# Query and key projections: the last 64 rows' high products of two tiles as one pair of half-height matmuls

## The chip, the cores and the metric

The kernel runs on one core of a Trainium2 chip. The metric is the device time of one launch in microseconds, as the median of several runs. A profiled execution of the same kernel gives the trace from which all durations below are taken.

## The reference, cut to what matters

Two independent computations stand side by side in the output, `[2048, 2 x 576]`. The left half is an attention with a compressed memory over four segments of 512 positions; the right half is a two-dimensional Fourier transform written as matrix products.

```python
# A: x [1, 2048, 576], H = 32 heads of Dh = 18, N = 4 segments of L = 512
q, k, v = x @ wq, x @ wk, x @ wv            # split by head and segment
for s in range(N):
    p = softmax(qs @ ks.T * scale + mask)   # mask: -1e9 where key > query
    a_dot = p @ vs
    a_mem = phi(qs) @ M / (phi(qs) @ z + 1e-6)   # phi(t) = t + 1 or exp(t)
    outs.append(g * a_mem + (1 - g) * a_dot)
    M = M + phi(ks).T @ vs;  z = z + phi(ks).sum()
A = concat(outs) @ wo
# B: real part of the transform along both axes
a, b = x2 @ dft_hid_re.T, x2 @ dft_hid_im.T
B = dft_seq_re @ a - dft_seq_im @ b
```

Everything is float32. The change touches the first line alone, the products for q and k.

## The kernel before

**Two parts to a number.** A float32 operand is cut in two: a high part rounded to the format that TensorE reads in one pass (`F32R`), and a low part, the rest. A product of two operands is then three matmuls: high x high, high x low and low x high. ScalarE (`act`) makes the high part, VectorE (`dve`) or GpSimd (`pool`) subtracts for the low one.

**Projections.** The contraction is 576 rows long: four blocks of 128 rows and a tail of 64. q and k are made transposed, in nine tiles of 128 features for each segment (`m` 0 to 3 are q, 4 to 7 are k, 8 holds the last 64 features of both), each tile 128 x 512 in one PSUM bank. A tile is a chain of 14 matmuls (`qk_terms`, L221): 3 for each of the four blocks, and 2 for the tail. The 64 tail rows lie twice in the 128 partitions, once in the upper and once in the lower half. `x_tail` holds high over low; the weights come as low over high (`W[2]`) and high over low (`W[3]`), so that the two matmuls of full height give all four products of the tail.

**Order of the work.** All instructions of an engine run in the order in which the program issues them, and `later(n, ...)` and `tick()` put steps behind. For each of the four segments:
- `open_qk(s)` (L237) runs tiles 0 to 3 side by side in four of the five banks of the tag `acc`, in groups of terms. In segment 0, where the inputs are still arriving, the groups are small; later there are two, terms 0 to 5 and 6 to 13. Between them stand the last sums of the memory (`accumulate`, L358).
- `memory()` (L367) copies the sums of the memory on ScalarE.
- `project_qk(s, m)` (L258) evacuates a tile or, for tiles 4 to 8, first runs its chain (`chain`, L82) in the next of the five banks. The order is 0 to 8 in segment 0 and 0, 1, 2, 3, 8, 4, 5, 6, 7 after that. To evacuate: for k, a copy kept for the memory (`kf`, L266, in segments 0 to 2); the first bfloat16 part `p` (ScalarE, L270); the rest `r` (VectorE, L271); for q, in later segments, `phi` with relu and exp (ScalarE, L214, L215), VectorE's L217 and L218 and GpSimd's L219. The second and third part of `p` (L280 to L283) follow one tick later. A bank comes free with its last reader.
- `project_v(s, j)` makes v in four blocks of positions, with two groups of matmuls each. In segments 0 to 2, between the two groups, TensorE transposes the copies of k (`k_natural`, kt at L300: tiles 8, 4, 5, and then 6 and 7). In segments 1 to 3 the lookups in the memory (`look`, L391 to L399) stand between them too.
- `split_x(s, k)` (L110) cuts the x of the next segment in two; `split_wk` (L119) does it for weights.

**The second part**, from about 220 us on, mixes the attention by heads with the dense products of the Fourier transform, and ends with the product with wo. The change does not touch it.

**Memory.** The pool `sk` lies on the right side of SBUF and is closed in the middle of segment 3, where `sr` takes its place.

Of the kernel before, what the change touches and what calls it, by code (L numbers as in the profile page):

```python
# [12 lines left out]
F32 = mybir.dt.float32  # L13
F32R = mybir.dt.float32r
F16 = mybir.dt.float16
BF16 = mybir.dt.bfloat16
AF = mybir.ActivationFunctionType
OP = mybir.AluOpType
AX = mybir.AxisListType.X
PSUM = bass.MemoryType.PSUM  # L20
DRAM = bass.MemoryType.DRAM

S, D, H, DH, NSEG, L = 2048, 576, 32, 18, 4, 512
P = 128
# [16 lines left out]
def infini_attention_and_fnet(ctx: ExitStack, tc: tile.TileContext, xT, wqk, w8, wv, wo, beta, xtT, cT, hT, out):  # L41
    nc = tc.nc
    act, dve, pool, pe = nc.scalar, nc.vector, nc.gpsimd, nc.tensor
# [14 lines left out]
    def split(hi, lo, raw, lo_engine=None):  # L58
        act.activation(hi, raw, AF.Copy)
        (lo_engine or dve).tensor_tensor(lo, raw, hi.bitcast(F32), OP.subtract)  # L60
# [19 lines left out]
    def chain(o, terms):  # L80
        for n, (a, b) in enumerate(terms):
            pe.matmul(o, a, b, start=n == 0, stop=n == len(terms) - 1)  # L82
# [3 lines left out]
    def later(n, fn, *a):  # L86
        due.setdefault(clock[0] + n, []).append((fn, a))
# [8 lines left out]
    sk = p1k.enter_context(tc.tile_pool(name="sb1k", bufs=1, side="right", reuse_waits="tile"))  # L96
    sb = p1.enter_context(tc.tile_pool(name="sb1", bufs=1, reuse_waits="tile"))
    ps = p1.enter_context(tc.tile_pool(name="ps1", bufs=2, space=PSUM))
# [11 lines left out]
    def split_x(s, k):  # L110
        raw = XR.pop((s, k))
        if k < 4:
            split(X[s][0][k], X[s][1][k], raw)
        else:
            t = X[s][2]
            act.activation(t, raw, AF.Copy)
            dve.tensor_tensor(t[64:], raw[64:], t[64:].bitcast(F32), OP.subtract)

    def split_wk(w, k, raw, wait=0):  # L119
# [14 lines left out]
    def load_w(src, cols, k):  # L134
        raw = sb.tile([P, cols], F32, name="raw", tag="raw", bufs=5)
        dma(raw, src[k])
        return raw

    def weight(mk):
        return [[mk() for _ in range(4)] for _ in range(2)] + [mk() for _ in range(2)]  # L140

    def wide_tile(cols):
        return lambda: wide.tile([P, cols], F32R, name="wide", tag="wide")

    WQ = weight(wide_tile(L))
    x_early = [[[sb.tile([P, L], F32R, name=f"x{n}{k}{i}") for k in range(2)] for n in "hl"] for i in range(2)]
    x_late = [[sb.tile([P, L], F32R, name=f"x{n}{k}") for k in (2, 3)] for n in "hl"]
    x_tail = sb.tile([P, L], F32R, name="xt")
    X = [(x_early[s % 2][0] + x_late[0], x_early[s % 2][1] + x_late[1], x_tail) for s in range(NSEG)]

    load_x(0, 0)
    raw = sb.tile([P, L], F32, name="raw", tag="raw", bufs=5)
# [6 lines left out]
    for k in range(1, 5):  # L159
        load_x(0, k)  # L160
        raw = load_w(wqk[:, :, :L], L, k)
# [3 lines left out]
    WK, WV = weight(wide_tile(L)), weight(wide_tile(D))  # L165
    for k in range(5):
        if k < 2:
            raw = sb.tile([P, L], F32, name="r", tag="r", bufs=3)
            dma(raw, wqk[k, :, L:])
        else:  # L170
            raw = load_w(wqk[:, :, L:], L, k)
# [40 lines left out]
    def phi(e, sources, hi, lo):  # L212
        for to, src in sources:
            act.activation(to, src, AF.Relu, scale=-1.0)  # L214
        act.activation(e, e, AF.Exp, scale=-1.0)  # L215
        for to, src in sources:
            dve.scalar_tensor_tensor(to, src, 0.0, to, op0=OP.max, op1=OP.add)  # L217
        dve.tensor_copy(hi, e)  # L218
        pool.tensor_tensor(lo, e, hi.bitcast(F32), OP.subtract)  # L219

    def qk_terms(s, m):  # L221
        xh, xl, xt = X[s]
        W, c = (WQ, m) if m < 4 else (WK, m - 4) if m < 8 else (W8, 0)
        cs = slice(c * P, (c + 1) * P)
        terms = []
        for k in range(4):
            terms += [(W[0][k][:, cs], xh[k]), (W[0][k][:, cs], xl[k]), (W[1][k][:, cs], xh[k])]
        return terms + [(W[2][:, cs], xt), (W[3][:, cs], xt)]

    FIRST, KF = {}, {}  # L230

    def warm_up():
        o = ps.tile([P, L], F32, name="warm", tag="acc", bufs=5)
# [3 lines left out]
    def open_qk(s):  # L237
        for m in range(4):
            FIRST[m] = ps.tile([P, L], F32, name="qk", tag="acc", bufs=5)
        terms = [qk_terms(s, m) for m in range(4)]  # L240
        edges = (0, 6, 14) if s else (0, 1, 2, 3, 6, 9, 14)
        for a, b in zip(edges, edges[1:]):
            for m in range(4):
                for n in range(a, b):
                    pe.matmul(FIRST[m], *terms[m][n], start=n == 0, stop=n == 13)  # L245
                if s and m == 0 and a:
                    accumulate(3, (1,))
            if s and a == 0:
                accumulate(3, (0,))
# [8 lines left out]
    def project_qk(s, m):  # L258
        if m in FIRST:
            o = FIRST.pop(m)  # L260
        else:
            o = ps.tile([P, L], F32, name="qk", tag="acc", bufs=5)
            chain(o, qk_terms(s, m))
        if m >= 4 and s < 3:
            KF[m] = sk.tile([P, L], F32, name="kf", bufs=5)
            act.activation(KF[m], o, AF.Copy)  # L266
        p = sb.tile([P, 3, L], BF16, name="p", tag="p", bufs=5)
        r = sb.tile([P, L], F32, name="r", tag="r", bufs=3)
        p0, p1, p2 = (p[:, 2 - i] if 4 <= m < 8 else p[:, i] for i in range(3))
        act.activation(p0, o, AF.Copy)  # L270
        dve.tensor_tensor(r, o, p0, OP.subtract)  # L271
        if s and (m < 4 or m == 8):
            n = P if m < 4 else 64
            c = m if m < 4 else 4
            e = sb.tile([P, L], F32, name="qe", bufs=2)[:n]
            phi(e, ((e, o[:n]),), pq_hi[:n, c], pq_lo[:, c] if m < 4 else pq_hi[64:, c])

        def rest():
            if m in (5, 6, 7):
                pool.tensor_copy(p1, r)  # L280
            else:
                act.activation(p1, r, AF.Copy)
            pool.tensor_tensor(p2, r, p1, OP.subtract)  # L283
            if m < 8:
                later(1, dma, (qd if m < 4 else kd)[s][(m % 4) * P:(m % 4 + 1) * P, :3], p)
            else:
                later(1, dma, qd[s][4 * P:, :3], p[:64])
                for i in range(3):
                    later(1, dma, kd[s][4 * P:, 2 - i], p[64:, i])

        later(1, rest)
# [12 lines left out]
    def project_v(s, j, meanwhile):  # L304
        xh, xl, xt = X[s]
        js = slice(j * P, (j + 1) * P)
# [36 lines left out]
    def accumulate(j, which=(0, 1)):  # L343
        (kh, kl), v = kn[j % 2], vn[j % 2]
        for n in which:
            for c in range(5):
                b, at, both = SUMS[c]
                o = sums(c)
                fs = slice(64 + c * P, 64 + (c + 1) * P) if c < 4 else slice(0, 64)
                hs = slice(HEAD0[c] + 8 - o.shape[2], HEAD0[c] + 8)  # L350
                if n:
                    todo = ((kl, v[:, 0, hs], o[:, 0]),)
                elif both:
                    todo = ((kh, v[:, :, hs], o),)
                else:
                    todo = ((kh, v[:, i, hs], o[:, 0]) for i in range(2))
                for keys, values, to in todo:
                    pe.matmul(to, keys[:, fs], values, start=b not in started, stop=True, skip_group_check=True)  # L358
                    started.add(b)
# [135 lines left out]
    for s in range(NSEG):  # L495
        more = s < 3
        if s == 0:
            warm_up()
        open_qk(s)
        if s:  # L500
            memory()
        else:
            tick()
        for n, m in enumerate((0, 1, 2, 3, 8, 4, 5, 6, 7) if s else range(9)):
            project_qk(s, m)
            tick()
            if not more and n in (5, 7):
                h_split(0, (n - 5) // 2)
            if s and n < 8:
                copy_parts(s - 1, 2 * n)  # L510
                copy_parts(s - 1, 2 * n + 1)
            if s in (1, 2) and n >= 4:
                load_x(s + 1, n - 4)
            if not more and n == 0:
                for k in range(5):
                    h_load(0, k)
            if not more and n == 4:
                p1k.close()
                sr = ctx.enter_context(tc.tile_pool(name="sb2r", bufs=1, side="right", reuse_waits="tile"))
                attention_tiles()  # L520
            if not more and n == 4:
                c_load(0)
                c_load(1)
                stacks(sr, 0)
                stack_load(0)
            if not more and n == 6:
                c_load(2)
# [26 lines left out]
    ps = ctx.enter_context(tc.tile_pool(name="ps2", bufs=2, space=PSUM, reuse_waits="tile"))  # L554
# [445 lines left out]
    for t in range(NT):  # L1000
# [3 lines left out]
        for h in range(2):  # L1004
            cs = slice(h * 288, h * 288 + 288)
            o = ps.tile([P, 288], F32, name="d", bufs=3)
            terms = []
# [5 lines left out]
            if h or t == NT - 1:  # L1013
                cs = cs if t == NT - 1 else slice(0, D)
# [45 lines left out]
```

## Time and profile before

| | |
|---|---|
| median of 3 runs | 999.67 us (999.23 to 1004.48) |
| profiled execution | 1000.37 us, its span 998.6 us |
| granted TensorE clock | 0.999 |
| TensorE busy | 989.0 us of the span |
| VectorE, ScalarE, GpSimd busy | 753.9, 710.9, 635.5 us |

A row of the profile names the engine, the line, and output<-inputs with their shapes. PE is a matmul, PEld the load of its weights, DVE is VectorE, ACT is ScalarE and POOL is GpSimd. In a timeline the columns are start and duration in us; a bracket gives the idle time of the engine ahead of the instruction, and who ended it. Several instructions of one kind may be merged in a row (x2). The segments' openings start at 5.1, 58.1, 112.9 and 169.6 us.

### The profile page before, as it was taken

The numbers are of one execution on the slowest core, as the hardware profiler recorded it, in microseconds if no ns is written. First come the engines' busy times: TensorE is split into PE (matmuls) and PEld (weight loads), VectorE is DVE, ScalarE is ACT, GpSimd is POOL, SyncE is SP. The second block draws the span as 40 slices with busy tenths as digits, with TensorE's granted clock in tenths as the row PEclk, the third lists the DMA queues.
The fourth block names the chain that finished last, engine by engine and source line by source line (L and its number), as shares of the span: only waits on it lengthen the run. The fifth ranks groups of instructions, "written<-read, shape, count | busy, mean of one in ns | idle before, by whom it ended". The sixth has DMA issues, their size and how long they took to land.

```text
span 998.6 us, 25575 instructions
## 1 busy us (share of the span) xinstructions
PE 989.0 (99%) x9291; PEld 923.7 (93%) x9291; DVE 753.9 (75%) x2048; ACT 710.9 (71%) x1677; POOL 635.5 (64%) x700
## 2 busy tenths in 40 slices
PE   9999999999999999999999999999999999999998
PEld 7988989898999999999999999999999999999998
DVE  6657668594678777878898888898888899998321
ACT  6667576663887877878788788877767777777243
POOL 2657576686767667666766777776767767767000
PEclk9999999999999999999999999999999999999999
DMA  7447556787578898899999887789999999899555
GB/s 254 161 131 231 205 177 238 236 306 214 138 169 204 208 230 210 209 229 217 254 228 247 220 208 198 181 197 223 223 239 214 242 237 243 228 202 189 137 152 138
DMA packets 305182, 208.92 MB, mean 209 GB/s; under 512 B 206240, under 2 KB 259872, under 8 KB 305056
## 3 DMA queue, kind: packets, MB, share of 16 engines
q1 hardware_dynamic: 304816, 207.15, 80.2%
q8 instruction: 73, 1.20, 0.5%
q14 instruction: 53, 0.43, 0.1%
q10 hardware_dynamic: 240, 0.14, 0.1%
HBM read 121.32 MB, written 57.93 MB: 180 GB/s over the span
## 4 chain that ended last, share of the span: by engine, by line
PE 89%; DVE 3%; DMA 3%; ACT 2%; POOL 2%; issue 1%; SPq 0%; POOLq 0%; DVEq 0%; ACTq 0%
PE d L572 39%; PE s L733 7%; PE d L82 6%; PE v L82 6%; PE pv L851 4%; PE qk L245 4%; PE qk L82 3%; PE d L617 3%; PE d L618 3%; PE d L619 3%; PE pv L852 2%; PE m L358 1%; PE t L807 1%; PE look L391 1%; PE t L810 1%
## 5 line engine op out<-in xcount | busy, mean ns | idle before, releaser
L739 DVE CUSTOM_DVE_ANT_0 s<-s,causal 128x128 f32<-128x128 f32 (+3 forms) x512 | 249.8, 498 | 101.1 <-PE s L733 92.0
L451 POOL TENSOR_TENSOR clo<-craw,chi 128x512 fp32r<-128x512 f32 x158 | 215.9, 1366 | 96.6 <-ACT chi L446 68.0
L572 PE MATMUL d<-wide,chi 128*128 128x288 f32 x1408 | 266.2, 306 | 0.4 <-DVE y L642 0.4
L572 PEld LDWEIGHTS d<-wide,chi 128*128 128x128 f32 x1408 | 211.8, 189 | 2.4 <-DVE y L642 0.6
L572 PE MATMUL d<-wide,clo 128*128 128x288 f32 x704 | 177.6, 319 | 0.0
L773 POOL TENSOR_TENSOR hl<-pf,hl 128x768 f16<-128x768 f32 x64 | 112.7, 1761 | 69.8 <-ACT hl L769 53.9
L733 PE MATMUL s<-ks,qs 108*128 108x128 bf16 (+3 forms) x512 | 133.7, 304 | 1.9 <-DVE negm L739 1.7
L819 ACT ACTIVATE phi<-t 128x384 f16<-128x384 f32 x128 | 61.7, 482 | 103.2 <-PE t L816 103.0
L762 ACT ACTIVATE pf<-s,nb 128x128 f32<-128x128 f32 (+3 forms) x256 | 128.1, 526 | 6.2
L834 DVE TENSOR_TENSOR plo<-pf,phi 128x384 f16<-128x384 f32 (+1 forms) x128 | 126.8, 991 | 0.0
L572 PE MATMUL d<-ab,chi 128*128 128x288 f32 x640 | 126.0, 306 | 0.0
L572 PEld LDWEIGHTS d<-wide,clo 128*128 128x128 f32 x704 | 118.6, 189 | 1.6
L446 ACT ACTIVATE chi<-craw 128x512 fp32r<-128x512 f32 x160 | 100.2, 627 | 5.8 <-DMA craw<-xtT 2.5
L820 ACT ACTIVATE pf<-t 128x384 f32<-128x384 f32 (+1 forms) x192 | 99.5, 518 | 6.2 <-PE t L807 6.0
L572 PEld LDWEIGHTS d<-ab,chi 128*128 128x128 f32 x640 | 98.5, 189 | 0.6
L769 ACT ACTIVATE hl<-pf 128x768 f16<-128x768 f32 (+1 forms) x128 | 87.4, 730 | 2.0
L572 PE MATMUL d<-ab,clo 128*128 128x288 f32 x320 | 84.8, 314 | 0.0
L617 PE MATMUL d<-wide,chi 128*128 128x288 f32 x256 | 84.0, 328 | 0.0
L619 PE MATMUL d<-wide,clo 128*128 128x288 f32 x256 | 75.6, 295 | 0.0
L618 PE MATMUL d<-wide,chi 128*128 128x288 f32 x256 | 75.6, 295 | 0.0
L773 DVE TENSOR_TENSOR hl<-pf,hl 128x512 f16<-128x512 f32 x64 | 67.6, 1056 | 0.1
L834 POOL TENSOR_TENSOR plo<-pf,phi 128x384 f16<-128x384 f32 x64 | 59.4, 928 | 13.0 <-ACT pf L820 10.4
(203 smaller groups left out, 2497.9 us busy)
## 6 DMA issues: line engine op xcount, KB each, us to landing
craw<-cT SPq DMA_DIRECT2D x128, 256.0 KB
ks<-kd SPq DMA_DIRECT2D x32, 432.0 KB
qs<-qd SPq DMA_DIRECT2D x32, 432.0 KB
craw<-xtT SPq DMA_DIRECT2D x32, 320.0 KB
vd<-vs SPq DMA_DIRECT2D x16, 440.0 KB
vst<-vd SPq DMA_DIRECT2D x32, 220.0 KB
qd<-p SPq DMA_DIRECT2D x16, 384.0 KB
kd<-p SPq DMA_DIRECT2D x16, 384.0 KB
```

Of the source, the lines that this page charges most:

```text
L82: pe.matmul(o, a, b, start=n == 0, stop=n == len(terms) - 1)
L446: act.activation(hi, raw[:, :4], AF.Copy)
L451: engine.tensor_tensor(lo, raw[:, :4], hi.bitcast(F32), OP.subtract)
L572: pe.matmul(o[h], a, b[:, h * 288:h * 288 + 288], start=start, stop=stop)
L617: pe.matmul(o, xh[:, k], wl[k][:, cs], start=k == 0, stop=False)
L618: pe.matmul(o, xh[:, k], wh[k][:, cs], start=False, stop=False)
L619: pe.matmul(o, xl[:, k], wh[k][:, cs], start=False, stop=False)
L733: pe.matmul(o[:, c:c + w], q[:, i * P:w], k[:, :w], start=True, stop=True)
L739: dve.tensor_tensor_reduce(o[:, c:c + w], o[:, c:c + w], CAUSAL[0][:, L - w:], scale=scale, scalar=-LOWEST, op0=OP.add, op1=OP.min, accum_ ...
L762: act.activation(f[:, FIRST_COL[i]:FIRST_COL[i] + w], o[:, c:c + w], AF.Exp, bias=nb[:, i:i + 1], scale=-1.0)
L773: engine.tensor_tensor(hl[:, 1, a:b], f[:, a:b], hl[:, 0, a:b], OP.subtract)
L834: (pool if kind == 2 else dve).tensor_tensor(lo[:, a:b], f[:, a:b], hi[:, a:b], OP.subtract)
```

## The change

For tiles 0 to 7 the second tail matmul is dropped as a matmul of full height. Its high x high product is formed with 64 rows instead: for the even tile of a pair in the upper half of the array (`W[3]` and `x_tail`, rows 0 to 63), for the odd tile in the lower half (`W[2]` and `x_under`, rows 64 to 127). The two stand next to each other in the program and write to different banks. The product low x low of the tail is left out for these tiles. `x_under` is a new tile in `sk` that holds the high part of the tail in its lower half; ScalarE copies it for each segment.

In `open_qk` the pair comes after the odd tile's other terms, so tile 0 ends together with tile 1, and 2 together with 3. For tiles 4 to 7 of segments 0 to 2 the pair comes first, ahead of the even tile's 13 other terms; the odd tile's bank is taken at the same time, and its 13 terms follow when its turn comes. In segment 3 the tiles 4 to 7 run as before, with 14 terms, and tile 8 does so in every segment.

```diff
@@ split_x
             act.activation(t, raw, AF.Copy)
+            act.activation(x_under[64:], raw[64:], AF.Copy)
             dve.tensor_tensor(t[64:], raw[64:], t[64:].bitcast(F32), OP.subtract)
@@
+    x_under = sk.tile([P, L], F32R, name="xu")
@@
+    def qk_tails(s, ms, o, first):
+        for n, m in enumerate(ms):
+            W, c = (WQ, m) if m < 4 else (WK, m - 4)
+            cs = slice(c * P, (c + 1) * P)
+            rows, w, x = (slice(64, P), W[2], x_under) if n else (slice(0, 64), W[3], X[s][2])
+            pe.matmul(o[n], w[rows, cs], x[rows], start=first, stop=not first)
+
+    FIRST, KF, PAIRED = {}, {}, set()
+
+    def finish(o, terms):
+        for n in range(13):
+            pe.matmul(o, *terms[n], start=False, stop=n == 12)
@@ open_qk
-                for n in range(a, b):
-                    pe.matmul(FIRST[m], *terms[m][n], start=n == 0, stop=n == 13)
+                for n in range(a, min(b, 13)):
+                    pe.matmul(FIRST[m], *terms[m][n], start=n == 0, stop=False)
+                if b == 14 and m % 2:
+                    qk_tails(s, (m - 1, m), (FIRST[m - 1], FIRST[m]), False)
@@ project_qk
             o = FIRST.pop(m)
+            if (s, m) in PAIRED:
+                finish(o, qk_terms(s, m))
         else:
             o = ps.tile([P, L], F32, name="qk", tag="acc", bufs=5)
-            chain(o, qk_terms(s, m))
+            terms = qk_terms(s, m)
+            if m in (4, 6) and s < 3:
+                FIRST[m + 1] = ps.tile([P, L], F32, name="qk", tag="acc", bufs=5)
+                qk_tails(s, (m, m + 1), (o, FIRST[m + 1]), True)
+                finish(o, terms)
+                PAIRED.add((s, m + 1))
+            else:
+                chain(o, terms)
```

More of the change, by code (lines that the diff above doesn't have):

```diff
@@ L228, in qk_terms @@
         return terms + [(W[2][:, cs], xt), (W[3][:, cs], xt)]
-    FIRST, KF = {}, {}
+    def qk_tails(s, ms, o, first):
[8 more added lines that the diff above has]
+            pe.matmul(o, *terms[n], start=False, stop=n == 12)
     def warm_up():
```

## The prediction

> **What bounds the kernel now.** I read the page first: its engines and the chain of work that ended last.
>
> ```profile
> PE 989.0 (99%) x9291; PEld 923.7 (93%) x9291; DVE 753.9 (75%) x2048; ACT 710.9 (71%) x1677; POOL 635.5 (64%) x700
> PE 89%; DVE 3%; DMA 3%; ACT 2%; POOL 2%; issue 1%; SPq 0%; POOLq 0%; DVEq 0%; ACTq 0%
> PE d L572 39%; PE s L733 7%; PE d L82 6%; PE v L82 6%; PE pv L851 4%; PE qk L245 4%; PE qk L82 3%; PE d L617 3%; PE d L618 3%; PE d L619 3%; PE pv L852 2%; PE m L358 1%; PE t L807 1%; PE look L391 1%; PE t L810 1%
> ```
>
> TensorE is busy throughout and carries 89% of the chain; the lines that are changed (qk at L245 and L82) carry 7%. Busy matmuls overlap in these records, so the next question was whether TensorE really never waits while the projections run. The waits of PE in the first 300 us answer that, and the table of windows does for what follows:
>
> ```profile
> PE warm L235 <- POOL ident L64: 1.4, 1, 1.4
> ...
> PE kt L300 <- ACT kf L266: 0.2, 1, 0.2
> 220.00:935.00 715.00, 712.02 (x7527) 668.65 (x7525) 590.97 (x1714) 543.73 (x1298) 495.83 (x550) 1.00 0.88 213
> ```
>
> After 220 us TensorE is busy for 712.02 of 715.00 us, so I let whatever the projections gain or lose pass one to one to the end. Within the projections there is one wait that looks like nothing, 0.2 us, for a copy by ScalarE (kf, L266). The argument turns on it.
>
> **What is saved: the pace of a tail matmul.** Segment 0's first tiles (timeline, PE), and the answer on the tile qk:
>
> ```profile
> 15.75 0.61 PE L245 MATMUL qk<-xt,wide 128*128 128x512 f32 x2
> ...
> 16.88 0.62 PE L245 MATMUL qk<-xt,wide 128*128 128x512 f32 x2
> ```
> ```profile
> L245 PEld LDWEIGHTS qk<-xt,wide x32: 187/188/188, 15.5 to 183.3; 128*128 128x128 f32 x32
> L245 PE MATMUL qk<-xt,wide x32: 389/389/396, 15.7 to 183.5; 128*128 128x512 f32 x32
>   ACT kf L266: 2.6, 2
> ```
>
> From 15.75 to 16.88 lie five matmuls (two tails, three full terms): 1.13 / 5 = 0.226 us each. A record lasts 0.389 us, so 0.163 us of it lies under the next one. The load of weights, 0.188 us, fits under a matmul too. Today two tiles have four tail matmuls; afterwards they have two of full height and two of half height in different halves. If those two overlap completely, a pair of tiles saves 0.226 us. There are 2 pairs in each of four segments from the opening, and 2 more in segments 0 to 2: 14 pairs, 14 x 0.226 = 3.16 us. That is 0.32% of the time: the most the change can give by itself, and less than the 0.5% that a measurement of this kernel can tell from no change.
>
> **What a change of height may cost.** No row of this trace has a 64-row matmul. The nearest thing is the sums of the memory, whose last piece has weights 64 columns wide, followed by full matmuls. Segment 1, PE:
>
> ```profile
> 64.27 0.61 PE L358 MATMUL m<-vn,knl 128*128 128x152 f32 x5
> 64.71 0.47 PE L245 MATMUL qk<-xh,wide 128*128 128x512 f32 x1
> 65.02 0.40 PE L245 MATMUL qk<-xl,wide 128*128 128x512 f32 x1
> ...
> 66.17 0.62 PE L245 MATMUL qk<-xt,wide 128*128 128x512 f32 x2
> ```
>
> The first full matmul behind them takes 65.02 - 64.71 = 0.31 us instead of 0.226: 0.08 us more, and its record is 0.47 instead of 0.389, the same 0.08. Narrow moving blocks contribute to that, so it is a stand-in. Call the cost of one switch d; each pair has two. Lower end 0: the next load and matmul slip under the last as they do everywhere else. Going below 0 is excluded, since a switch takes no work away. Upper end: the array empties (0.163) and only then loads weights (0.188): 0.35. I take 0.08, the row that is nearest in kind. A pair then changes TensorE's work by 2 x 0.08 - 0.226 = -0.066 us, 14 pairs by -0.9 us.
>
> [...]
>
> **Segment 0** has nothing against the saving. The new copy on ScalarE (x_under, priced as the xt copy in the next rows, 0.63 us) goes ahead of the tail weights' copies:
>
> ```profile
> 11.99 0.63 ACT L116 ACTIVATE xt<-kf 128x512 fp32r<-128x512 f32 x1
> 12.62 1.15 ACT L128 ACTIVATE wide<-raw 128x512 fp32r<-128x512 f32 x2
> ```
> ```profile
> 14.19 0.69 DVE L125 TENSOR_TENSOR wide<-raw,wide 64x512 fp32r<-64x512 f32 x1
> ```
>
> The last tail weights are ready at 14.88 now and about 15.5 then; the first tail matmul is at 15.75, so 0.2 us of cover is left. ScalarE itself catches up later, for it waits 2.6 us in two places for qk's matmuls (the kf row above). In later segments the copy falls into the 4.19 us in which ScalarE is idle at the opening (next rows). Segment 0: 4 x -0.066 = -0.3 us.
>
> **Segments 1 and 2: the saving meets ScalarE.** Here is the new wait. Tile 0's evacuation (p, L270) now needs tile 0's last product, which is issued with tile 1's, one tile later. ScalarE and then PE in segment 1:
>
> ```profile
> 64.87 1.19 ACT L367 ACTIVATE mf<-m 128x152 f32<-128x152 f32 x5 [4.19 <-PE m L358]
> 65.96 0.58 ACT L270 ACTIVATE p<-qk 128x512 bf16<-128x512 f32 x1
> 67.30 0.60 ACT L214 ACTIVATE qe<-qk 128x512 f32<-128x512 f32 x1 [0.76 <-DVE r L271]
> ...
> 88.07 0.62 ACT L266 ACTIVATE kf<-qk 128x512 f32<-128x512 f32 x1
> ```
> ```profile
> 88.74 0.33 PE L300 MATMUL kt<-ident,kf 128*128 128x128 f32 x1 [0.18 <-ACT kf L266]
> 89.04 0.45 PE L391 MATMUL look<-md,pq_hi 128*128 128x152 f32 x2
> ```
>
> Today ScalarE starts tile 0 at 65.96, straight behind the memory's copies, while TensorE is already in tile 1. From there p, r on VectorE, relu, exp and the next p follow each other with waits only on one another, until kf of tile 7 at 88.07 to 88.69, and TensorE's transpose kt stands waiting for exactly that (0.18 us). Where ScalarE's row waits, it waits for VectorE, never for a projection. So the lag of ScalarE is 22.1 us long, fixed at its head, and it decides when TensorE goes on. Afterwards: tile 0 loses its second tail, the pair starts where tile 1's first tail stands now, 66.17, and ends at 66.17 + 0.39 = 66.56 (plus d). Tile 0's p moves from 65.96 to 66.56: +0.60 us, with d +0.68. Everything behind it on ScalarE (relu, exp, all later tiles) moves with it, kf of tile 7 too, and kt starts 0.68 us later, measured from the segment's start. TensorE's own saving in the four pairs only lengthens its wait. Segment 2 has the same picture, ScalarE and PE:
>
> ```profile
> 122.72 0.58 ACT L270 ACTIVATE p<-qk 128x512 bf16<-128x512 f32 x1
> ...
> 144.79 0.62 ACT L266 ACTIVATE kf<-qk 128x512 f32<-128x512 f32 x1
> ```
> ```profile
> 144.72 1.07 PE L300 MATMUL kt<-ident,kf 128*128 128x128 f32 x5
> ```
>
> The same 22.07 us from p to the last kf, which ends at 145.41 inside the five transposes. Two segments: +0.68 each.
>
> The early second bank for tiles 5 and 7 is another wait, with the matmuls behind it in PE's queue. It asks for tile 3's bank at about 79.77 - 3 x 0.066 = 79.6 in segment 1, by these rows:
>
> ```profile
> 78.19 0.69 DVE L217 SCALAR_TENSOR_TENSOR qe<-qk,qe 128x512 f32<-128x512 f32 x1 [1.46 <-ACT qe L215]
> ```
> ```profile
> 79.77 0.39 PE L82 MATMUL qk<-xh,wide 128*128 128x512 f32 x1
> ```
>
> That bank comes free at 78.88 + 0.68 = 79.56. It just fits; if it does not, the loss is swallowed by the longer wait at kt.
>
> **Segment 3** has no kt, but its second group of v takes the bank that tile 7's r frees. ScalarE, VectorE, PE:
>
> ```profile
> 179.46 0.58 ACT L270 ACTIVATE p<-qk 128x512 bf16<-128x512 f32 x1
> ```
> ```profile
> 203.51 0.68 DVE L271 TENSOR_TENSOR r<-qk,p 128x512 f32<-128x512 f32 x1
> ```
> ```profile
> 204.65 0.47 PE L82 MATMUL v<-wide,xh 128*128 128x288 f32 x2
> ```
>
> The bank is free at 204.19 and wanted at 204.65, a slack of 0.46. A shift of 0.68 leaves +0.22; TensorE's two pairs alone would give -0.13. I take +0.2.
>
> **Sum:** -0.3 + 0.68 + 0.68 + 0.2 = +1.3 us. The profiled execution took 1000.37 us (span 998.6, so 1.8 us around it), 0.70 above the median of the runs, 999.67. By its own time 1001.7; against the median 1001.0, which I predict.
>
> **Rivals.**
> *The switch empties the array and exposes the load* (d = 0.35, the upper end). Place: both edges of each pair. A pair costs 0.70 - 0.226 = +0.47 us. Segment 0: 4 x 0.47 = 1.9; segments 1 and 2: TensorE becomes the later one again, 1.9 - 0.18 = 1.7 each; segment 3: 0.95. Together +6.3: 1006.0 us. It decides from about d = 0.31, where the sum passes 5.0 us (0.5%). Against it: the stand-in of 0.08. For it: nothing here shows a load prefetched across such an edge. Chance 0.25. [...]
>
> *The halves do not overlap* (the change does not do what it says): the pair costs what two tails cost now plus 2d = +0.16. Segment 0 +0.64, segments 1 and 2 still +0.68 by ScalarE, segment 3 +0.3: +2.3, so 1002.0. Chance 0.13. [...]
>
> *The saving comes through*: ScalarE's lag shrinks elsewhere (VectorE's and GpSimd's steps on its path have some play), and kt does not come later. With d = 0.08 it is -0.9, 998.8; with d = 0 it is -3.2, 996.5. Against it: the trace's 22.1 us twice over. Chance 0.12.
>
> **How the numbers follow.** Forecast (1001.0; from +0.4 us at d = 0 to +2.2 at d = 0.163, so 1000.1 to 1001.9) 0.47, the rivals 0.25, 0.13 and 0.12, something unseen 0.03. The range 998.2 to 1006.8 takes in the forecast, the rival without overlap, half of the third rival and most of the first. Slower by over 0.5% (beyond 1004.7): the first rival and part of the unseen, with some room for an outlying median, 0.28. Faster by over 0.5% (below 994.7) needs more than the whole saving: 0.03. The rest, 0.69.
>
> **What would show it.** In the changed profile, the two 64-row matmuls of a pair start nearly together, and from the pair's start to the full matmul behind it pass 0.25 to 0.4 us; 0.45 and more means no overlap, 0.6 and more the costly switch. In segments 1 and 2 ScalarE's first p starts about 0.6 us later behind the memory's copies, now waiting for PE, and the wait of kt for kf grows from 0.2 us to about 1 us per segment. The lag from that p to the last kf stays at 22.1 us. Wrong would be: no wait at kt, or a segment 0 that gets longer.

## The result and the profile after

| | before | after |
|---|---|---|
| median of 21 runs each | 1000.75 us (998.98 to 1004.48) | 1002.63 us (1001.58 to 1004.61) |
| profiled execution, its span | 1000.37, 998.6 us | 1003.64, 1001.9 us |

The ratio is 1.0018, with a 95% interval of 1.001 to 1.0027: the kernel became slower by 1.8 us (1.0 to 2.7). Beside the experiments further down the kernel before had medians of 999.0 to 999.3 us, not 1000.75, so their ratios can be compared with this one only roughly (e1_tall has 1.0037); the argument goes by stages of the profiles.

The page of the changed kernel has the chain of work that ended last spread over more engines than before: TensorE 85% instead of 89%, ScalarE 4% instead of 2%.

```profile
PE 85%; DVE 4%; ACT 4%; DMA 3%; POOL 2%; issue 1%; SPq 0%; POOLq 0%; DVEq 0%; ACTq 0%
```

**The pair itself** (the answer on line 238 with its matmuls of 64 rows, then the timeline of TensorE and of its weight loads in segment 1):

```profile
L238 PE MATMUL qk<-xt,wide x14: 392/498/498, 17.0 to 185.4; 64*128 64x512 f32 x14
L238 PE MATMUL qk<-xu,wide x14: 394/491/495, 17.0 to 185.4; 64*128 64x512 f32 x14
```
```profile
66.28 0.39 PE L259 MATMUL qk<-xt,wide 128*128 128x512 f32 x1
66.60 0.50 PE L238 MATMUL qk<-xt,wide 64*128 64x512 f32 x1
66.60 0.49 PE L238 MATMUL qk<-xu,wide 64*128 64x512 f32 x1
67.03 0.50 PE L259 MATMUL qk<-xh,wide 128*128 128x512 f32 x1
67.36 0.39 PE L259 MATMUL qk<-xl,wide 128*128 128x512 f32 x1
```
```profile
66.06 0.19 PEld L259 LDWEIGHTS qk<-xt,wide 128*128 128x128 f32 x1
66.59 0.18 PEld L238 LDWEIGHTS qk<-xt,wide 64*128 64x128 f32 x1 [0.35 <-issue]
66.60 0.18 PEld L238 LDWEIGHTS qk<-xu,wide 64*128 64x128 f32 x1
67.02 0.19 PEld L259 LDWEIGHTS qk<-xh,wide 128*128 128x128 f32 x1 [0.24 <-issue]
```

The two halves do start together and overlap in full. But both edges cost. Between the last full matmul and the pair pass 0.32 us instead of 0.226, and the loads do not begin before that time is over: the queue of loads stands still for 0.35 us. The pair's records are 0.11 us longer than 0.389, which I read as the part of the load that lies open. Behind the pair it is the same again: 0.43 us to the next full matmul, whose record is 0.50 too, and 0.33 us to the one after it. From 66.28 to 67.36 pass 1.08 us. Before, these were four slots of 0.226, 0.904 us. A pair costs 0.17 us more than what it replaces, and one switch d = (1.08 - 3 x 0.226) / 2 = 0.20 us: about 0.09 us more before the next matmul starts and 0.11 us of open load. The 0.09 is a shorter overlap: as far as the modelled ends of matmul records can tell, the last full matmul (to 66.67) and the pair (from 66.60) still overlap by 0.07 us, instead of by 0.163. What holds the pair back for that time is not shown.

**Where tile 0 ends** (timeline of ScalarE, segment 1, its first p and its last kf, and TensorE's kt):

```profile
64.98 1.19 ACT L392 ACTIVATE mf<-m 128x152 f32<-128x152 f32 x5 [3.20 <-PE m L383]
67.13 0.60 ACT L295 ACTIVATE p<-qk 128x512 bf16<-128x512 f32 x1 [0.97 <-PE qk L238]
...
89.15 0.62 ACT L291 ACTIVATE kf<-qk 128x512 f32<-128x512 f32 x1
```
```profile
89.83 0.33 PE L325 MATMUL kt<-ident,kf 128*128 128x128 f32 x1 [0.24 <-ACT kf L291]
90.13 0.45 PE L416 MATMUL look<-md,pq_hi 128*128 128x152 f32 x2
```

ScalarE now waits 0.97 us for the pair (L238), where p used to follow the memory's copies at once. From there to the last kf pass 22.02 us, before 22.11. The wait of kt that the profile shows is 0.24 us.

To see the stages by themselves I measure each segment from its first qk matmul to that of the next, segment 3 to the first scores. (Segment 1 opens at 56.2 us in the kernel before, not at 58.1 as the section on the profile has it.) Segment 0 is measured from the first tail matmul to the first of v, since its start depends on when the inputs land: in the profiles of all the kernels here the first tail matmul stands anywhere between 14.4 and 15.7 us.

| us | segment 0 | segment 1 | segment 2 | segment 3 | 1 to 3 |
|---|---|---|---|---|---|
| before | 19.72 | 56.76 | 56.74 | 50.32 | |
| after | +0.33 | +0.77 | +0.79 | +0.78 | +2.34 |

The second part, from the first scores on, is 0.6 us longer in the profile of after. Most of that is one wait at its beginning, the first of these rows (the second is kt's wait in segments 1 and 2 together):

```profile
PE trm L815 <- POOL mb L811: 1.2, 1, 1.2
PE kt L325 <- ACT kf L291: 0.5, 2, 0.2
```

The first wait was 0.7 us before. In the experiments below it lies between nothing and 2.2 us, whether segments 1 to 3 are long or short, so I don't count it as the change's.

### The profile page after: what moved, and what is told of

Same layout as the page of the kernel before. It is cut to its first block, busy times and chain, and to the rows that moved or that the text cites. A ratio compares the mean times of both kernels' runs of the same rounds, so it can differ in the third digit from the quotient of the medians.

```text
span 1001.9 us, 25582 instructions
## 1 busy us (share of the span) xinstructions
PE 991.6 (99%) x9291; PEld 920.2 (92%) x9291; DVE 753.2 (75%) x2048; ACT 714.0 (71%) x1681; POOL 635.1 (63%) x700
## 4 chain that ended last, share of the span: by engine, by line
PE 85%; DVE 4%; ACT 4%; DMA 3%; POOL 2%; issue 1%; SPq 0%; POOLq 0%; DVEq 0%; ACTq 0%
PE d L597 38%; PE s L758 7%; PE d L82 6%; PE v L82 5%; PE pv L876 4%; PE qk L259 4%; PE d L642 3%; PE d L643 3%; PE d L644 3%; PE pv L877 2%; PE t L832 1%; PE m L383 1%; PE qk L244 1%; PE look L416 1%; DVE r L296 1%
```

## The experiments

The theory: two prices. A visit to half height, from a full-height matmul over to half-height ones and back, costs TensorE two switches of 0.20 us; and tile 0 ends late, which ScalarE's lag carries through segments 1 to 3. The rival: TensorE's price is all there is; 14 x 0.17 us = 2.4 us would explain the total just as well. The label before each expectation is the name of the run in the table at the end of this section. The edits are shortened to their main lines.

**e1_tall: the order without the array mode.**

```diff
-            rows, w, x = (slice(64, P), W[2], x_under) if n else (slice(0, 64), W[3], X[s][2])
-            pe.matmul(o[n], w[rows, cs], x[rows], start=first, stop=not first)
+            pe.matmul(o[n], W[3][:, cs], X[s][2], start=first, stop=not first)
```

> The changed kernel's order of matmuls, with every matmul at full height again (both members of a pair read W[3] and x_tail with 128 rows; the low x low product of the tail is back). Nothing visits half height, tile 0 still ends together with tile 1. Theory (two causes: about 0.40 us of TensorE per visit to half height, and the late end of tile 0 that ScalarE's fixed lag carries through segments 1 to 3): segment 0 unchanged, the second part begins +0.6 +0.6 +0.3 = about +1.5 us later than in the kernel before, and tile 0's p starts +0.6 us later in each segment. Rival (all of it is TensorE's price, 14 pairs at +0.17 us): 0.0 us.

Measured: ratio 1.0037 (1.0023 to 1.0051); segments 1 to 3 +1.84 us. With not one matmul of half height, nearly four fifths of the change's loss in these segments are there. ScalarE shows it:

```profile
66.88 0.60 ACT L294 ACTIVATE p<-qk 128x512 bf16<-128x512 f32 x1 [0.76 <-PE qk L237]
```

The wait for the pair is 0.76 us instead of 0.97; the 0.2 us between them is the switch. Segment 0 missed its 0: +0.84 us. There the early pair of tiles 4 and 5 reads all of the weight tail, and TensorE waits for VectorE's part of it, which the half-height version doesn't read. The wait is shown as 0.6 us. The four matmuls of the two pairs take 1.75 us with it (18.58 to 20.33) instead of four slots, 0.90, which is all of the 0.84:

```profile
18.58 0.61 PE L237 MATMUL qk<-xt,wide 128*128 128x512 f32 x2
19.79 0.70 PE L237 MATMUL qk<-xt,wide 128*128 128x512 f32 x2 [0.60 <-DVE wide L126]
20.33 0.39 PE L243 MATMUL qk<-xh,wide 128*128 128x512 f32 x1
```

**e2_open_only and e3_late_only: the change in two halves.**

```diff
 # e2_open_only
-            if m in (4, 6) and s < 3:
+            if False:
 # e3_late_only: open_qk as in the kernel before
-                for n in range(a, min(b, 13)):
-                    pe.matmul(FIRST[m], *terms[m][n], start=n == 0, stop=False)
-                if b == 14 and m % 2:
-                    qk_tails(s, (m - 1, m), (FIRST[m - 1], FIRST[m]), False)
+                for n in range(a, b):
+                    pe.matmul(FIRST[m], *terms[m][n], start=n == 0, stop=n == 13)
```

> The pairs of the openings alone (8 pairs); tiles 4 to 7 run their 14 full matmuls as before. Theory: segment 0 +0.35 us, segments 1 to 3 about +0.8 us each through tile 0's p: second part +2.7 us, as late as with all 14 pairs. Rival (TensorE's price alone): 8 x 0.17 = +1.4 us.

> The pairs of tiles 4 to 7 alone (6 pairs); the openings are as before, so tile 0 ends when it did. Theory: tile 0's p does not move; segment 0 +0.35 us, segments 1 and 2 +0.34 less the 0.18 that TensorE waited at kt anyway, +0.16 each, segment 3 nothing: second part +0.7 us. Rival (TensorE's price alone): 6 x 0.17 = +1.0 us.

Measured: the openings alone, ratio 1.0033 (1.0023 to 1.0044), segments 1 to 3 +2.38 us, all of the change's loss there. The late pairs alone, ratio 1.0009 (0.9998 to 1.0019), segments 1 to 3 +0.05 us: the timed runs don't tell it from the kernel before. The rival wanted 1.0 and 0.7 us for these segments (6 and 4 pairs at 0.17). In the run with the late pairs ScalarE's p stands behind the memory's copies as ever, and TensorE, which comes to kt 0.34 us later, has no wait for kf left there:

```profile
64.97 1.19 ACT L390 ACTIVATE mf<-m 128x152 f32<-128x152 f32 x5 [3.19 <-PE m L381]
66.06 0.58 ACT L293 ACTIVATE p<-qk 128x512 bf16<-128x512 f32 x1
```
```profile
88.40 0.78 PE L323 MATMUL kt<-ident,kf 128*128 128x128 f32 x5
89.16 0.45 PE L414 MATMUL look<-md,pq_hi 128*128 128x152 f32 x2
```

I had expected +0.16 in segments 1 and 2; it was +0.01. TensorE's own price vanishes there altogether. This run also has ScalarE's new copy of x_under in every segment, so that copy costs segments 1 to 3 nothing. Segment 0 became 0.98 us longer instead of 0.35. In this profile the first tail matmul stands at 14.87, 0.9 us earlier than in the kernel before, and the second one, of full height here, reads VectorE's part of the weight tail and waits for it. VectorE, then TensorE:

```profile
14.13 0.68 DVE L125 TENSOR_TENSOR wide<-raw,wide 64x512 fp32r<-64x512 f32 x1 [0.54 <-ACT wide L129]
14.84 0.69 DVE L126 TENSOR_TENSOR wide<-raw,wide 64x512 fp32r<-64x512 f32 x1
```
```profile
14.87 0.50 PE L259 MATMUL qk<-xt,wide 128*128 128x512 f32 x1
15.59 0.50 PE L259 MATMUL qk<-xt,wide 128*128 128x512 f32 x1 [0.22 <-DVE wide L126]
15.92 0.39 PE L259 MATMUL qk<-xh,wide 128*128 128x512 f32 x1
```

From 14.87 to 15.92 pass 1.05 us instead of two slots, 0.45: 0.60 us, and with the 0.35 of the two late pairs 0.95 of the 0.98. VectorE's part ends at 15.53, after a wait of 0.54 us for ScalarE, where the copy of x_under now stands ahead of the weights' copies. So here that copy does cost, because the tail matmuls come earlier; the change itself has no second tail matmul of full height at this place. How segment 0 lies to its inputs differs between executions: the run e4 below, without that copy, has +0.17 there with nothing changed in that segment.

**e4_act_pad: the lag alone, no matmul changed.**

```diff
+        if s and m == 0:
+            act.activation(pad, WQ[0][0], AF.Copy)
         act.activation(p0, o, AF.Copy)
```

> The kernel before with one useless ScalarE copy of 128 x 512 (about 0.6 us) ahead of tile 0's p in segments 1 to 3; not one matmul is changed or moved. Theory (ScalarE's lag decides when kt and the later groups go on): segments 1 and 2 +0.6 us each, segment 3 about +0.3: second part +1.5 us. Rival (only TensorE's work counts): 0.0 us.

Measured: ratio 1.0017 (1.0009 to 1.0026); segments +0.44, +0.47 and +0.75, together +1.66 us (the first two below the 0.6 that I had expected, the third above its 0.3). One copy that nobody reads, 0.53 us between its start and that of p, makes this kernel about as slow by the timed runs as the change was, and no matmul is different:

```profile
65.13 0.62 ACT L272 ACTIVATE pad<-wide 128x512 fp32r<-128x512 f32 x1
65.66 0.58 ACT L273 ACTIVATE p<-qk 128x512 bf16<-128x512 f32 x1
```

**e5_quad and e6_quad_alone: the same products in another place.** In segments 1 to 3 the four half-height matmuls of tiles 0 to 3 form one visit behind the memory's sums (e5_quad; segment 0 and tiles 4 to 7 as in the change; e6_quad_alone leaves these as in the kernel before). The old places of these matmuls fall away.

```diff
                 if s and m == 0 and a:
                     accumulate(3, (1,))
+                    for i in (0, 2):
+                        qk_tails(s, (i, i + 1), (FIRST[i], FIRST[i + 1]), False, (i == 0, False))
```

> All 14 pairs as in the change, but in segments 1 to 3 the four half-height matmuls of tiles 0 to 3 stand in one visit right behind tile 0's terms and the memory's sums, so that tile 0 ends before ScalarE has copied the memory. Theory (tile 0's late end is what costs in these segments): tile 0's p starts 0.2 us earlier than in the kernel before, counted from the segment's opening; segments 1 and 2 become longer by TensorE's +0.29 less the 0.18 that it waited at kt, +0.11 each, segment 3 by 0: from segment 1's opening to the second part +0.2 us, where the change has +2.3. Rival (a visit to half height costs the later stages in some other way, wherever it stands): +1.5 us or more stay.

> Only the one visit of four half-height matmuls in each of segments 1 to 3, as in the run with all pairs beside it; segment 0 and tiles 4 to 7 as before. Theory: the visit replaces four full matmuls (0.91 us) by two slots and two switches (0.45 + 0.40), -0.05 us of TensorE, and moves tile 0's p 0.2 us earlier: segments 1 and 2 -0.2 us each, segment 3 -0.05: -0.45 us to the second part, the best order of the half-height products, and too small for the timed runs to tell from the kernel before. Rival (the switch costs more where the visit is larger): +0.2 us or more for each segment.

Measured: e5_quad 0.999 (0.9981 to 0.9999), segments 1 to 3 -0.69 us; e6_quad_alone 0.9999 (0.999 to 1.0008), -0.64 us. TensorE and ScalarE of e5_quad:

```profile
63.54 0.50 PE L238 MATMUL qk<-xt,wide 64*128 64x512 f32 x1
63.54 0.49 PE L238 MATMUL qk<-xu,wide 64*128 64x512 f32 x1
63.88 0.39 PE L238 MATMUL qk<-xt,wide 64*128 64x512 f32 x1
63.88 0.39 PE L238 MATMUL qk<-xu,wide 64*128 64x512 f32 x1
64.20 0.50 PE L260 MATMUL qk<-xh,wide 128*128 128x512 f32 x1
```
```profile
63.61 1.19 ACT L395 ACTIVATE mf<-m 128x152 f32<-128x152 f32 x5 [2.80 <-PE m L386]
64.70 0.58 ACT L298 ACTIVATE p<-qk 128x512 bf16<-128x512 f32 x1
```

p follows the copies again without a wait. All 14 pairs are still there, with e5's late pairs adding 0.34 us of TensorE's time to segments 1 and 2, and yet the segments are shorter than in the kernel before, by what p gained in the opening (0.2 us each). My +0.2 for e5 was wrong by 0.9: I had let TensorE's 0.29 count, less 0.18. For e6 I had -0.45, with segment 3 at -0.05 where it gained 0.20. The second pair of a visit has records of 0.39. In the changed kernel's visit of two pairs in segment 0 the records are the same, 0.49 and then 0.39, and there the loads of the second pair start 0.23 us ahead of it (19.52 and 19.75), those of the first with it (both 19.41): as I read it, only the first has an open load. e5 is also faster than the kernel before by the timed runs, but by 0.1%, at the edge of the interval; only the 0.7 us of segments 1 to 3 are shown by stage.

**e7_solo: the price of a visit.**

```diff
+            if 4 <= m < 8 and s < 3:
+                terms[13] = (WK[3][:64, (m - 4) * P:(m - 3) * P], X[s][2][:64])
```

> The kernel before, but the last term of tiles 4 to 7 in segments 0 to 2 (12 tiles) is one half-height matmul without a partner, at the end of each tile's chain; low x low of the tail is left out. It has the price of a visit by itself. Theory (the price belongs to the visit, two switches of 0.20 us, whatever stands in it): each tile +0.40 us; segment 0 from tile 4's first matmul to the first of v +1.6 us, segments 1 and 2 +1.4 each after the 0.18 that TensorE waited at kt. Rival (the price belongs to each half-height matmul, a pair's 0.62 us shared by two): +0.08 us for each tile, +0.3 us in segment 0.

Measured: one run, 1002.35 us. Segment 0 from the first tail matmul to v: 21.32 instead of 19.72, +1.60, four times 0.40. The price belongs to the visit. In segment 1 kt begins +1.61 us later (90.48 us, against 87.96 and an opening that is 0.91 later), but the segment grows by 0.97 only:

```profile
90.48 0.71 PE L303 MATMUL kt<-ident,kf 128*128 128x128 f32 x5
90.94 0.43 PE L394 MATMUL look<-md,pq_hi 128*128 128x152 f32 x2
```

The five transposes take 0.46 us here until the lookups start. In the kernel before they take 1.08 at this place (87.96 to 89.04), and 0.46 in the next block of the same segment:

```profile
87.96 0.60 PE L300 MATMUL kt<-ident,kf 128*128 128x128 f32 x4
...
94.23 0.71 PE L300 MATMUL kt<-ident,kf 128*128 128x128 f32 x5
94.69 0.32 PE L391 MATMUL look<-md,pq_hi 128*128 128x152 f32 x1
```

So in the kernel before TensorE stands waiting for 0.62 us among these transposes, of which the profile shows 0.18, and it can come that much later for nothing: 1.61 - 0.62 is about the 0.97 measured. I had counted on 0.18 and expected +1.4.

**e8_head: the lag at its head.** In the kernel before, tile 0 is evacuated ahead of the memory's copies.

```diff
         if s:
+            project_qk(s, 0)
             memory()
...
-            project_qk(s, m)
+            if m or not s:
+                project_qk(s, m)
```

> The kernel before, no half-height matmul in it; in segments 1 to 3 tile 0's evacuation is issued ahead of the copies of the memory's sums, so ScalarE starts tile 0's p as soon as TensorE has finished the tile, about 1.5 us earlier (64.45 instead of 65.96 in segment 1). Theory (in these segments ScalarE's lag, fixed at tile 0, holds TensorE; the run with solo matmuls showed 0.6 us of play per segment between kt and the lookups): segments 1 and 2 become shorter by 0.6 us each, segment 3 by 0.2, -1.4 us to the second part, while TensorE's matmuls are the same in number and kind. Rival (TensorE alone sets the time of these segments): 0.0 us.

Measured: ratio 1.0079 (1.0065 to 1.0094); segments 1 to 3 +8.2 us. The sign of my forecast was wrong. Tile 0's p did start 1.5 us earlier counted from the opening, but the copies now stand behind its exp and wait there for VectorE and GpSimd, so that tile 1's p comes at 69.46, 1.6 us later than before (68.99, with an opening that is 1.09 earlier):

```profile
65.97 0.65 ACT L367 ACTIVATE mf<-m 128x152 f32<-128x152 f32 x3
67.50 0.30 ACT L367 ACTIVATE mf<-m 128x152 f32<-128x152 f32 x1 [0.88 <-DVE mf L369]
68.81 0.23 ACT L367 ACTIVATE mf<-m 64x76 f32<-64x76 f32 x1 [1.01 <-POOL mf L363]
68.94 0.62 ACT L282 ACTIVATE p<-r 128x512 bf16<-128x512 f32 x1
69.46 0.58 ACT L270 ACTIVATE p<-qk 128x512 bf16<-128x512 f32 x1
```

The rival's 0.0 is refuted all the same: with the same matmuls, a later evacuation costs the segments several microseconds. How short they become with a lag that is shorter by more than e5's and e6's 0.2 us was not settled by it.

| us against before | segment 0 | 1 | 2 | 3 | 1 to 3 |
|---|---|---|---|---|---|
| the change | +0.33 | +0.77 | +0.79 | +0.78 | +2.34 |
| e1_tall | +0.84 | +0.60 | +0.62 | +0.62 | +1.84 |
| e2_open_only | +0.35 | +0.78 | +0.79 | +0.81 | +2.38 |
| e3_late_only | +0.98 | +0.01 | +0.01 | +0.03 | +0.05 |
| e4_act_pad | +0.17 | +0.44 | +0.47 | +0.75 | +1.66 |
| e5_quad | +0.33 | -0.24 | -0.25 | -0.20 | -0.69 |
| e6_quad_alone | 0.00 | -0.21 | -0.23 | -0.20 | -0.64 |
| e7_solo | +1.60 | +0.97 | +0.99 | 0.00 | +1.96 |
| e8_head | 0.00 | +3.72 | +2.27 | +2.25 | +8.24 |

## Why the prediction held, and where it did not

**The mechanism held.** The forecast was a small loss, because the saving is at most 0.32%, and because tile 0's late end would cost segments 1 and 2 more than TensorE gains there. The halves overlapped as the forecast took it (the two halves of each of the 14 pairs start within 5 ns of each other; the 0.43 us from the pair's start to the full matmul behind it are over the 0.25 to 0.4 that I had named for that and do not tell it by themselves); tile 0's p moved by 0.84 us from the opening (+0.68 forecast), its lag stayed at 22.0 us, and the segments grew by 0.77 and 0.79 (+0.68 each). The runs e1, e2, e4 and e5 show that the late end of tile 0, carried on by ScalarE, makes the loss of segments 1 to 3. Most of it is the order (e1, +1.84 of 2.34); the rest is the switch ahead of the pair, which makes tile 0 end 0.2 us later still.

**The term that was mis-sized is d.** I took 0.08 us from full matmuls behind narrow weights; a switch costs 0.20, inside my bounds of 0 and 0.35. As I read it, the stand-in lacked the 0.09 us ahead of the matmul and had only part of the open load (its record is 0.08 us longer, a pair's 0.11). So a pair is a loss by itself, +0.17 us instead of -0.066, and segment 0 became longer by 0.33 us, not shorter by 0.3. I had named a longer segment 0 as what would prove me wrong, and it does so for this term. With d = 0.20 four pairs in four visits would give 4 x 0.17 = 0.68; tiles 2, 3 and 4, 5 stand next to each other there and share a visit, which saves one, 0.40: 0.28 against the measured 0.33. The rival of the costly switch named an emptied array and an open load, 0.35 together, and would have decided from 0.31 on. Measured are 0.09 us more before a matmul starts and 0.11 us more in its record; that the array empties was an estimate, and no run shows it. The rival without overlap named +2.3 us, nearer to what was measured than the forecast, but its mechanism is refuted: the halves start together, and a matmul without a partner costs the same visit (e7).

**Segment 3** was +0.78 us instead of +0.2. I had priced the bank that tile 7 leaves, and in the change it did not hold TensorE, which came there 0.35 us later by its own two pairs. What I had not seen is a later wait. Before the lookups of the third block of v TensorE was late by 0.44 us, and there it waits for VectorE's rest of the block before. VectorE's step for it in the kernel before and after, then the lookup before and after:

```profile
211.09 0.81 DVE L322 TENSOR_TENSOR vr<-v,vs 128x288 f32<-128x288 f32 x2
213.76 0.81 DVE L347 TENSOR_TENSOR vr<-v,vs 128x288 f32<-128x288 f32 x2
```
```profile
211.62 0.42 PE L391 MATMUL look<-md,pq_hi 128*128 128x152 f32 x2
214.25 0.45 PE L416 MATMUL look<-md,pq_hi 128*128 128x152 f32 x2 [0.15 <-DVE vr L347]
```

Counted from the opening, VectorE's step comes 0.79 us later in the change, 0.64 in e1, 0.77 in e4 and 0.23 us earlier in e5: in each run about what the segment gained or lost. (In e4 ScalarE's lateness grows from 0.47 to 0.75 us in this segment, at a wait of 1.15 us for VectorE behind tile 2 that is 0.88 in the kernel before; why is not shown.) So the lag of the evacuation sets segment 3 too, with ScalarE and VectorE late to the same amount, and TensorE's 0.34 us lie inside it.

**The wait at kt** did not grow to 1 us for each segment. It shows 0.24 us. From kt's start to the lookups pass 1.14 us (88.99 to 90.13) instead of 1.08, so with 0.46 for the transposes TensorE waits 0.68 us after 0.62. The wait hardly grew, because TensorE itself comes 0.69 us later by its four pairs, where I had it come earlier; and most of it was never shown. Reading those 0.18 us as all of TensorE's play was the mistake that also spoilt my numbers for e3, e5 and e7.

**The sum** was +1.3 us; by stage it is +2.67 up to the second part (0.33 + 2.34), and by the timed runs +1.8 (1.0 to 2.7). The measured 1002.63 us lie above the forecast's own band, 1000.1 to 1001.9, and inside the range only because that was drawn up to 1006.8 for the costly switch (the band ends at d = 0.163, the overlap of two records taken as the price of a switch; no run shows that price, a switch cost 0.20); 1.1 us of the distance to 1001.0 is that the kernel before had 1000.75 in these runs and not 999.67. Segments 1 and 2 were forecast by their cause; that the total came out near is partly luck of a wide range.

## What to carry to other kernels

Before matmuls are paired in half-height tiles, count the visits and not the matmuls: here each visit cost 0.40 us, so one pair lost 0.17 us and only two pairs in one visit lost nothing (1.32 us from 19.09 to 20.41 in segment 0, where six slots of 0.226 are 1.36). When terms are moved, look at when each output is finished and who starts on it: a tile that ended 0.6 to 0.8 us later cost as much again in each segment, since the engine that evacuates ran a fixed lag behind TensorE and decided when TensorE could go on. Here a busy TensorE whose profile showed a wait of 0.18 us had 0.62 us in play, time by which it could come later for nothing; adding a known amount of work (e3, e7) measures it, and so does the same group of instructions at a place where nothing waits.

## What the runs showed of the hardware

Both weight loads of a pair start within 5 ns of each other, and so do its matmuls. Among the full-height matmuls of these tiles a load starts 0.22 us ahead of its own matmul, under the one before it (66.06 and 66.28); at both edges of a visit load and matmul start together (66.59 and 66.60, 67.02 and 67.03). A half-height matmul without a partner costs the same visit as a pair, 0.40 us (e7_solo, four tiles, +1.60 us). Of the one pass in which TensorE reads `F32R` the kernel before shows this: a 128x512 product of such operands is one record of 0.389 us, a 108x512 product of bfloat16 (s, L733) one of 0.391. Between the profiles of these kernels the first tail matmul moved by 1.4 us and the length of the second part by 2.4 us; differences of this size were read by stage and not from single spans.
